# A gated recurrence and a two-way maxout layer on one core: three directly loaded blocks instead of four, single-block chunks, and the first stores sent later

## The chip, the core and the metric

The kernel runs on one core of one Trainium2 chip. Its time is the device time of one execution in microseconds (us). The kernel before the change has a median of 397.41 us over five runs, which lie between 396.77 and 397.58.

A core has five engines with a queue of instructions each: TensorE (PE in the profile, with the loading of weights as PEld), VectorE (DVE), ScalarE (ACT), GpSimd (POOL) and SyncE (SP, which here only issues DMAs). Each works through its queue in order and waits where an operand isn't there yet.

## What is computed

```python
sig = 1 / (1 + exp(-f_logit))
f = lower_bound + (1 - lower_bound) * sig        # 4 x 6144 x 256
for t in range(6144):
    h = f[:, t] * h + (1 - f[:, t]) * x[:, t]
    y[:, t] = h
out = maximum(y @ w1, y @ w2) @ w_out            # w1, w2: 256 x 1024, w_out: 1024 x 256
```

All inputs and the output are float32. The recurrence runs over the tokens of each of the four batches and each of 256 channels by itself. The second part works token by token on 24576 tokens.

## The kernel before

**Arithmetic.** The maximum is written as `relu(y @ (w2 - w1)) @ w_out + y @ (w1 @ w_out)`, so that each token needs one hidden product instead of two. With `u = sigmoid(-f_logit)` the forget factor is `1 - (1 - lower_bound) * u`, and the input of the recurrence is `u * x`; the factor `1 - lower_bound` is put into the weights. The prepared weights are `wd` (the difference), `wob` (`w_out` in bf16) and `w13` (the product of `w1` and `w_out`).

**Blocks.** A block is 512 tokens; there are 48, twelve in each batch. The recurrence wants the channels on the partitions and the tokens along the free dimension, so both inputs have to be turned. A block then needs: `u` by ScalarE (gate), `v = u * x` by VectorE (drive), the forget factors for two halves of 128 channels (forget), a scan for each half on VectorE, eight hidden products of 128 units (each two matmuls with 512 columns), eight relus on ScalarE, and the projection, 40 matmuls with 256 columns, with copies and stores of the result in two pieces.

**Two ways in.** The first `NP = 4` blocks are loaded as float32 by SP (`load`), gated and driven in their natural layout, and turned by TensorE (`turn_pe`, 16 transposes for a block). All later blocks go in chunks of `CB = 2` blocks. `cast` makes a bf16 copy of f_logit and of x in one of two scratch buffers in DRAM, with two DMAs issued on POOL. `turn_dma` reads them back turned, with two transposing DMAs on SP, into tiles of 2 x 1024 elements in each partition. `cast_behind` puts one small POOL copy from the turned f into `held`, which waits for that turn, and issues the next chunk's cast behind it. So casts and turns of successive chunks form one chain.

**Order.** Nothing reorders the work: the order in the source is the order in each engine's queue. `LOADS` is the order of the loads. `PLAN` is the hand-written prologue. Its items are: G gate, V drive, TU and TV turns on TensorE, F forget, S scan, RW and RO rounding of weights, D difference, SC scaling, TW and KW turns of w1, W and KL the product `w13`, H hidden, R relu, P a step of the projection, L its linear steps, O copy out, `warm` products that only keep TensorE busy; then the block and unit, the half of the block (a or b), and behind a dot the engine. `CA` at its end issues chunk 0, and the cast of chunk 1 behind it. Outputs of the prologue are copied by O and sent by `send_pending` as soon as chunk 0's turns have been issued.

The loop follows, for blocks j from 3 to 48 and eight steps fc: the hidden product of block j, and an eighth of the projection of block j - 1. At (j, 0) and (j, 4) `store` copies and sends a piece of an earlier block. At the places in `gate_of` the recurrence of a later block is put in, and at those in `turn_of` a chunk's turns and the next cast.

SP's queue therefore holds the loads, the first turns, and then stores and turns in the order of the loop; a turn behind a store waits until VectorE has made that store's copy.

Of the kernel before, what the change touches and what calls it, by code (L numbers as in the profile page):

```python
# [16 lines left out]
def kernel(  # L17
# [22 lines left out]
    NQ = TB // P  # L40
    NBB = S // TB
    NBLK = B * NBB
    NP = 4
    CB = 2
    assert NBB % CB == 0 and NP % CB == 0
    NCH = (NBLK - NP) // CB
    NS = 2

    const = ctx.enter_context(tc.tile_pool(name="const", bufs=1))
# [8 lines left out]
    midpool = ctx.enter_context(tc.tile_pool(name="mid", bufs=2))  # L58
    ypool = ctx.enter_context(tc.tile_pool(name="ypool", bufs=4))
    rpool = ctx.enter_context(tc.tile_pool(name="rpool", bufs=3 * FC))  # L60
    opool = ctx.enter_context(tc.tile_pool(name="opool", bufs=8))
    lastpool = ctx.enter_context(tc.tile_pool(name="last", bufs=2))
    PS = bass.MemoryType.PSUM
    ps_d = ctx.enter_context(tc.tile_pool(name="ps_d", bufs=5, space=PS))
# [100 lines left out]
    }  # L165

    def cast(c):
        b, k = divmod(NP + c * CB, NBB)
        for name, src in (("fs", f_logit), ("xs", x)):
            nc.gpsimd.dma_start(  # L170
                out=spare[c % NS, name][:],
                in_=src[b, k * TB : (k + CB) * TB, :],
                max_dma_last_dim=4096,
            )

    def turn_dma(c):
        for s, name in enumerate(("fs", "xs")):
            t = ttpool.tile([P, KC, CB * TB], BF16, name=("fT", "xT")[s])
            turned[c, s] = t
            nc.sync.dma_start_transpose(out=t[:], in_=spare[c % NS, name][:])  # L180

    def cast_behind(c):

        if c + 1 < NCH:
            last = CB * TB - 1
            nc.gpsimd.tensor_copy(out=held[:], in_=turned[c, 0][:, KC - 1, last : last + 1])  # L186
            cast(c + 1)

    def part(j, s):
        c, o = divmod(j - NP, CB)  # L190
        return turned[c, s][:, :, o * TB : (o + 1) * TB]

    def gate(j):
# [125 lines left out]
    def send_out(j, g):  # L319
        r0 = j * TB + 2 * g * P  # L320
        nc.sync.dma_start(
            out=out[r0 : r0 + 2 * P, :].rearrange("(p r) d -> p r d", r=2),
            in_=osbs[j, g][:],
        )

    def store(j, g):
        copy_out(j, g)
        send_out(j, g)

    def store_row(j, g, r):  # L330
        osb = lastpool.tile([P, D], FP32, name="row")
# [111 lines left out]


    LOADS = """
    f0a x0a f0b w13 w23 x0b w12 w22 wo3 w10 w20 w11 wo2 w21 f1a x1a wo0 f1b x1b wo1
    f2a f2b x2a x2b f3 x3
    """
    PLAN = """
    G0a RW3.p keeps_T keeps V0a TU0a D31.p warm3 TV0a D30.p G0b F0a0.v warm4 TU0b  # L450
    D21.p F0a1.v S0a1 S0a0 V0b F0b1.a warm1 TW3 F0b0.a RW0.p warm5 TV0b RW2.v S0b1
    D01.p KW3.a TW2 SC31.a SC30.a KW2.a S0b0 RO3.a H06a H07a D20.v SC21.a warm3 H06b
    SC20.v H07b D00.v W133 RW1.v R07.a TW0 H04b H04a RO2.p H05a R06.a P071 SC00.v
    H05b P070 P061 D10.p TW1 SC01.a KW0.v R05.a R04.v H01a KW1.v H00a H00b H01b P040
    P050 P060 G1a P041 SC10.v V1a W132 R01.a D11.p TU1a RO0.p SC11.a P051 TV1a R00.a
    H02a F1a1.v F1a0.a RO1.p H03b S1a1 P011 G1b H02b S1a0 P010 H03a R02.a W130 V1b
    P001 R03.a TU1b H17a F1b1.v P000 TV1b H15a F1b0.a S1b1 S1b0 G2a H16a P031 P030
    P021 G2b W131 KL1.v TU2a F2a0.a P020 H17b H15b KL0.v H16b L01 L11 R17.a TU2b
    H10a H10b R16.a V2a R15.v F2a1.v H11b O01.a P161 H11a TV2a F2b0.a H12b P151 L10
    P171 V2b H12a R11.a F2b1.v R10.a S2a1 TV2b S2a0 G3b P150 R12.a S2b1 G3a L00 S2b0  # L460
    H13a V3b TU3b O00.a H13b P101 R13.a F3b1.v H14a P160 F3b0.v H14b P100 P170 H20
    H26 V3a TU3a P111 F3a1.v H21 R14.a H27 R20.a F3a0.v R26.a TV3a S3a1 P120 H24
    TV3b R21.a P121 P110 S3a0 H22 R27.a S3b1 P130 R24.a R22.a S3b0 H23 P131 R23.a
    H25 P140 O10.v P141 R25.a O11.v CA
    """

    engines = {"a": nc.scalar, "v": nc.vector, "p": nc.gpsimd}
# [10 lines left out]

    outs = []

    def send_pending():

        while outs and turned:
            send_out(*outs.pop(0))

    def issue(item):
        name, _, e = item.partition(".")
        eng, on_dve, on_act = engines.get(e), e == "v", e == "a"
        kind = name.rstrip("0123456789ab")
        arg = ["ab".index(c) if c in "ab" else int(c) for c in name[len(kind) :]]  # L490
        if kind == "warm":
            keep_warm(arg[0])
        elif name == "keeps_T":
            turn_bound()
        elif name == "keeps":
            keeps()
        elif kind in ("G", "V") and len(arg) == 2:
            (gate_nat if kind == "G" else drive_nat)(arg[0], 2 * arg[1], 2 * arg[1] + 2)
        elif kind in ("TU", "TV"):
            turn_pe(arg[0], "UV".index(kind[1]), arg[1])  # L500
        elif kind == "F" and len(arg) == 3:
            j, x, h = arg
            tok = slice(x * HB, (x + 1) * HB)
            forget(ffs[j][:, h, tok], uT[j, x][:, h, :], h, on_act)
        elif kind == "S" and len(arg) == 3:
            j, x, h = arg
            scan(j, h, x * HB, (x + 1) * HB, vT[j, x][:, h, :])
        elif kind == "RW":
            round_w1(arg[0], eng)
        elif kind == "RO":  # L510
            round_wout(arg[0], eng)
        elif kind == "D":
            diff(arg[0], arg[1], eng)
        elif kind == "SC":
            scale(arg[0], arg[1], on_dve)
        elif kind == "TW":
            turn_w1(arg[0])
        elif kind == "KW":
            keep_w1(arg[0], eng)
        elif kind == "W":  # L520
            linear_weights(int(name[3]))
        elif kind == "KL":
            keep_linear(arg[0], on_dve)
        elif kind == "H":
            (hidden_half if len(arg) == 3 else hidden_whole)(*arg)
        elif kind == "R":
            relu(arg[0], arg[1], on_dve)
        elif kind == "P":
            pair_steps(arg[0], arg[2], [arg[1]])
        elif kind == "L":  # L530
            pair_steps(arg[0], arg[1], [FC, FC + 1])
        elif kind == "O":
            copy_out(arg[0], arg[1], on_act)
            outs.append(arg)
            send_pending()
        elif kind == "CA":
            nc.gpsimd.tensor_copy(out=held[:], in_=ins[2][1][:, 3, D - 1 : D])
            cast(0)
            turn_dma(0)
            cast_behind(0)  # L540
            send_pending()
        else:
            raise ValueError(item)


    turn_of = {(3, 5): 1, (5, 2): 2, (7, 0): 3}
    turn_of |= {divmod(FC * (NP + c * CB - 3) - 3, FC): c for c in range(4, NCH)}
    gate_of = {(3, 1): 4, (3, 6): 5, (4, 5): 6, (5, 3): 7, (6, 3): 8, (7, 1): 9}
    gate_of |= {(b - 2, 4): b for b in range(10, NBLK)}

    with tc.manual_schedule():
        for j in range(NP):
            alloc_in(j)
        nc.scalar.dma_start(out=lbr[:], in_=lower_bound.rearrange("(h p) -> h p", p=P))
        for name in LOADS.split():
            load_item(name)
        nc.vector.memset(warm[:], 0.0)  # L557
        make_identity(nc, ident[:])
        nc.vector.tensor_copy(out=ident_b[:], in_=ident[:])
        keep_warm(7)  # L560
        for item in PLAN.split():
            issue(item)
        assert not outs

        for j in range(3, NBLK + 1):
            for fc in range(FC):
                if j < NBLK:
                    hidden(j, fc)
                project(j - 1, fc)
                if fc == 0 and j > 3:  # L570
                    store(j - 2, 1)
                if fc == 4 and j < NBLK:
                    store(j - 1, 0)
                if j == NBLK and fc in (3, 5, 7):
                    if fc == 3:
                        store(j - 1, 0)
                    else:
# [41 lines left out]
```

## Time and profile before

The page describes one profiled execution on this core. That execution took 396.93 us; its span, from the first to the last instruction, is 395.2 us. A digit in a row of tenths is the busy share in a fortieth of the span.

| what | value |
|---|---|
| median of five runs | 397.41 us (396.77 to 397.58) |
| profiled execution | 396.93 us, span 395.2 us |
| granted TensorE clock | full in every stretch |
| bytes moved by DMA | 79.12 MB, mean 200 GB/s |
| plain DMAs and turns from SP (q1) | 56.9% of 16 engines' span |
| casts from POOL (q0) | 35.6% of 16 engines' span |

```profile
PE   7999999999999999999999999999999999999996
PEld 3896766667777776767777776767777776666775
DVE  4896875757755765676567556755775576567622
ACT  4787676676667666766776677667666766676661
POOL 2511011101001101101101011011011010100000
PEclk9999999999999999999999999999999999999999
DMA  7999999989999999999989999999898898981122
...
L240 ACT ACTIVATE rt<-dT 128x512 bf16<-128x512 f32 x382 | 223.1, 596 | 105.2 <-PE dT L245 102.1
L268 PE MATMUL psO<-wob,rt 128*128 128x256 bf16 x1536 | 231.0, 273 | 0.2
...
L245 PE MATMUL dT<-y,wd 128*128 128x512 bf16 x690 | 208.8, 379 | 2.2
L149 DVE TENSOR_TENSOR_SCAN y<-ff,y,v 128x512 bf16<-128x512 bf16 x82 | 105.2, 1283 | 2.9
```

In a row of a group stand the line, the engine, the operation, the tile written and those read, the count, then busy us and mean ns of one, and the idle time before them with what ended it. TensorE's rows show almost no idle time before them; those of ScalarE and VectorE do, and they wait for TensorE. The DMA row is high from the start until near the end.

### The profile page before, as it was taken

The page shows a single profiled execution, that of the slowest core. Times are in us where ns is not written, and L with a number is a line of the kernel's source. Part 1 is how long each engine was busy: PE and PEld are TensorE (multiplying, and loading weights), DVE is VectorE, ACT ScalarE, POOL GpSimd, SP SyncE. Part 2 cuts the span into 40 slices and gives each one's busy share as a digit, 9 for nine tenths or more (in the row PEclk, how much of TensorE's full clock was granted, in tenths as well). Part 3 has the DMA queues.
Part 4 walks back from the last instruction along what each step waited for, and adds up shares of the span by engine and source line. Part 5 has one row for each costly group of instructions (what it writes and reads, how often), then busy time and mean ns, then how long its engine had stood idle before and what let it go on. Part 6 is the DMA issues. An engine that isn't in the chain of part 4 may idle for free.

```text
span 395.2 us, 7146 instructions
## 1 busy us (share of the span) xinstructions
PE 387.2 (98%) x2793; PEld 274.4 (69%) x2840; DVE 251.5 (64%) x366; ACT 273.5 (69%) x451; POOL 37.7 (10%) x83
## 2 busy tenths in 40 slices
PE   7999999999999999999999999999999999999996
PEld 3896766667777776767777776767777776666775
DVE  4896875757755765676567556755775576567622
ACT  4787676676667666766776677667666766676661
POOL 2511011101001101101101011011011010100000
PEclk9999999999999999999999999999999999999999
DMA  7999999989999999999989999999898898981122
GB/s 249 350 244 196 225 219 197 247 182 204 210 230 219 212 221 224 226 234 192 207 197 208 182 219 189 223 216 188 199 211 205 187 201 196 216 188 55 53 81 107
DMA packets 125078, 79.12 MB, mean 200 GB/s; under 512 B 94194, under 2 KB 101620, under 8 KB 125044
## 3 DMA queue, kind: packets, MB, share of 16 engines
q1 hardware_dynamic: 113072, 55.59, 56.9%
q0 software_dynamic: 11968, 23.07, 35.6%
q8 instruction: 22, 0.36, 0.4%
q14 instruction: 12, 0.10, 0.1%
q10 hardware_dynamic: 4, 0.00, 0.0%
HBM read 53.48 MB, written 48.23 MB: 257 GB/s over the span
## 4 chain that ended last, share of the span: by engine, by line
PE 95%; DMA 1%; DVE 1%; issue 1%; SPq 1%; DVEq 0%
PE psO L268 53%; PE dT L245 39%; PE dT L225 2%; DMA xn<-in_x_dram 1%; PE dT L126 1%; SPq L100 0%; PE psO L413 0%; DVE vn L113 0%; SPq L344 0%; DVE y L149 0%; DVE wd L388 0%; DVE wdf L380 0%; DVE row L332 0%; PE dT L396 0%; DVEq L113 0%
## 5 line engine op out<-in xcount | busy, mean ns | idle before, releaser
L240 ACT ACTIVATE rt<-dT 128x512 bf16<-128x512 f32 x382 | 223.1, 596 | 105.2 <-PE dT L245 102.1
L268 PE MATMUL psO<-wob,rt 128*128 128x256 bf16 x1536 | 231.0, 273 | 0.2
L268 PEld LDWEIGHTS <-rt 128*128 128x128 bf16 x1536 | 150.0, 98 | 94.7
L245 PE MATMUL dT<-y,wd 128*128 128x512 bf16 x690 | 208.8, 379 | 2.2
L149 DVE TENSOR_TENSOR_SCAN y<-ff,y,v 128x512 bf16<-128x512 bf16 x82 | 105.2, 1283 | 2.9
L317 DVE COPY osb<-psO 128x512 f32<-128x512 f32 x93 | 62.7, 679 | 67.4 <-PE psO L268 67.4
L245 PEld LDWEIGHTS <-wd 128*128 128x128 bf16 x736 | 72.0, 98 | 8.7
L268 PE MATMUL psO<-w,y 128*128 128x256 bf16 x384 | 72.5, 273 | 0.0
L201 DVE TENSOR_TENSOR v<-u,xT 128x1024 bf16<-128x1024 bf16 x44 | 30.5, 692 | 60.7 <-ACT u L197 52.6
L197 ACT ACTIVATE u<-fT 128x1024 bf16<-128x1024 bf16 x44 | 46.2, 1049 | 1.9 <-DMA fT<-fs 1.9
L268 PEld LDWEIGHTS <-y 128*128 128x128 bf16 x384 | 37.6, 98 | 4.4
L186 POOL CAST held<-fT 128x1 f32<-128x1 bf16 x21 | 5.4, 256 | 279.9 <-DMA fT<-fs 279.9
L138 DVE TENSOR_SCALAR ff<-u,nom 128x512 bf16<-128x512 bf16 x88 | 29.7, 338 | 0.0
L170 POOL DMA_DIRECT2D fs<-in_f_logit_dram x22 | 12.3, 559 | 4.7 <-issue 4.7
L170 POOL DMA_DIRECT2D xs<-in_x_dram x22 | 12.2, 552 | 0.0
L149 DVE TENSOR_TENSOR_SCAN y<-nff,y,dT 128x256 bf16<-128x256 bf16 x14 | 9.6, 731 | 1.8 <-PE dT L126 1.3
L225 PE MATMUL dT<-y,wd 128*128 128x256 bf16 x64 | 10.1, 273 | 0.3 <-DVE wd L388 0.2
L433 PE MATMUL psO<-warm 128*128 128x512 bf16 x22 | 7.2, 459 | 1.2 <-DVE warm L557 1.2
L149 DVE TENSOR_TENSOR_SCAN y<-ff,v 128x512 bf16<-128x512 bf16 x6 | 7.3, 1225 | 0.2
L108 ACT ACTIVATE un<-fn 128x512 bf16<-128x512 f32 x8 | 5.0, 627 | 3.1 <-DMA fn<-in_f_logit_dram 2.9
L113 DVE TENSOR_TENSOR vn<-un,xn 128x512 bf16<-128x512 bf16 x8 | 6.1, 759 | 1.2 <-DMA xn<-in_x_dram 1.2
L225 PEld LDWEIGHTS <-wd 128*128 128x128 bf16 x64 | 5.8, 98 | 1.4 <-issue 0.4
(40 smaller groups left out, 51.2 us busy)
## 6 DMA issues: line engine op xcount, KB each, us to landing
out_dram<-osb SPq DMA_DIRECT2D x95, 256.0 KB, 3.0
fs<-in_f_logit_dram POOLq DMA_DIRECT2D x22, 512.0 KB, 6.4
xs<-in_x_dram POOLq DMA_DIRECT2D x22, 512.0 KB, 9.4
fn<-in_f_logit_dram SPq DMA_DIRECT2D x6, 256.0 KB, 6.0
xn<-in_x_dram SPq DMA_DIRECT2D x6, 256.0 KB, 5.6
w1n<-in_moe_w_dram SPq DMA_DIRECT2D x4, 256.0 KB, 5.6
w2n<-in_moe_w_dram SPq DMA_DIRECT2D x4, 256.0 KB, 5.9
won<-in_moe_w_out_dram SPq DMA_DIRECT2D x4, 256.0 KB, 6.0
```

The costliest lines, as they stand in the source:

```text
L113: nc.vector.tensor_tensor(out=vs[j][:, q0:q1, :], in0=us[j][:, q0:q1, :], in1=ins[j][1][:, q0:q1, :], op=ALU.mult,)
L138: nc.vector.tensor_scalar(out=o, in0=i, scalar1=nom[:, h : h + 1], scalar2=1.0, op0=ALU.mult, op1=ALU.add)
L149: nc.vector.tensor_tensor_scan(out=ys[j][:, h, t0:t1], data0=ffs[j][:, h, t0:t1], data1=v, initial=initial, op0=ALU.mult, op1=ALU.add,)
L170: nc.gpsimd.dma_start(out=spare[c % NS, name][:], in_=src[b, k * TB : (k + CB) * TB, :], max_dma_last_dim=4096,)
L197: nc.scalar.activation(out=us[j][:], in_=part(j, 0), func=AF.Sigmoid, scale=-1.0)
L201: nc.vector.tensor_tensor(out=vs[j][:], in0=us[j][:], in1=part(j, 1), op=ALU.mult)
L225: nc.tensor.matmul(dts[j, fc][:, tok], lhsT=wd[:, kc, unit(fc)], rhs=ys[j][:, kc, tok], start=(first and kc == 0), stop=(not first and kc ...
L240: nc.scalar.activation(out=rt[:], in_=dts[j, fc][:], func=AF.Relu)
L245: nc.tensor.matmul(dts[j, fc][:], lhsT=wd[:, kc, unit(fc)], rhs=ys[j][:, kc, :], start=(kc == 0), stop=(kc == KC - 1),)
L268: nc.tensor.matmul(ps, lhsT=lhsT, rhs=rhs, start=start, stop=stop, skip_group_check=True)
L317: nc.vector.tensor_copy(out=osbs[j, g][:], in_=pos[j, g, 0][:])
L433: nc.tensor.matmul(idle[:].rearrange("p r d -> p (r d)"), lhsT=warm[:, 0:P], rhs=warm[:], start=True, stop=True,)
```

## The change

- `NP` becomes 3. Block 3 is no longer loaded and turned by TensorE; it goes the way of the later blocks.
- `CHUNKS` lists the chunks: blocks 3, 4 and 5 as chunks of one block, then pairs from (6, 7) on. `cast`, `turn_dma` and `cast_behind` take the number of blocks from it. A single's turns fill the first 512 of the 1024 columns of their tile.
- `CA` now stands within `PLAN`, waits for x of block 1 and issues the cast and turns of chunk 0. `CB`, later in `PLAN`, issues the cast of chunk 1 behind them, and its turns. Behind `PLAN`, chunks 2 and 3 are cast and turned, and the cast of chunk 4 is issued, each behind the turned f of the chunk before.
- No store is sent in the prologue or at j = 3 and 4. The copies are put in a list, and from j = 5 on `send_pending` sends up to two of the oldest at (j, 0) and (j, 4). The pool of output tiles grows from 8 to 12.
- `LOADS` and `PLAN` are new orders. `turn_of` and `gate_of` are new for the first chunks. Chunks from (10, 11) on are turned at the same places in the loop as before.

```diff
-    NP = 4
+    NP = 3
     CB = 2
...
+    CHUNKS = [(NP + i, 1) for i in range(CB * 2 - 1)]
+    CHUNKS += [(b, CB) for b in range(2 * NP, NBLK, CB)]
...
-    opool = ctx.enter_context(tc.tile_pool(name="opool", bufs=8))
+    opool = ctx.enter_context(tc.tile_pool(name="opool", bufs=12))
...
     def cast(c):
-        b, k = divmod(NP + c * CB, NBB)
+        b0, n = CHUNKS[c]
+        b, k = divmod(b0, NBB)
         for name, src in (("fs", f_logit), ("xs", x)):
             nc.gpsimd.dma_start(
-                out=spare[c % NS, name][:],
-                in_=src[b, k * TB : (k + CB) * TB, :],
+                out=spare[c % NS, name][0 : n * TB, :],
+                in_=src[b, k * TB : (k + n) * TB, :],
                 max_dma_last_dim=4096,
             )
...
-            nc.sync.dma_start_transpose(out=t[:], in_=spare[c % NS, name][:])
+            nc.sync.dma_start_transpose(
+                out=t[:, :, 0 : n * TB], in_=spare[c % NS, name][0 : n * TB, :]
+            )
...
     def store(j, g):
         copy_out(j, g)
-        send_out(j, g)
+        outs.append((j, g))
...
     LOADS = """
+    f0a x0a w12 f0b x0b w22 w10 w20 wo2 w13 w23 w11 wo0 w21 f1a x1a f1b wo3 x1b wo1
+    f2 x2
     """
     PLAN = """
+    keeps_T D20.p G0a V0a TU0a warm1 TV0a RW2.a warm6 TW2 keeps G0b F0a0.v warm1
+    TU0b F0a1.v KW2.a F0b1.a S0a0 S0a1 V0b warm3 TV0b F0b0.a D21.v SC21.a SC20.a
+    RW0.a D00.p S0b1 D01.p S0b0 warm6 H04a RW3.p RO2.v H05a SC00.a H04b H05b R04.a
...
+    R02.a W133 KW1.a RO1.v P060 F1b0.a P071 CA TV1b S1b0 H14a H16a F1b1.a H13a W131
+    H15a KL1.a P020 S1b1 G2a G2b P031 P030 P021 H14b KL0.v CB H16b TU2a R14.v H13b
...
+    O01.a H17b P111 P151 H12b G3 P100 S2a0 S2b1 H12a P110 P130 L10 S2b0 V3 R17.a H24
+    R12.a R24.a H22 R22.a H20 H27 F31.v H23 R20.a F30.v S31 P140 H21 S30 H26 P120
+    R27.a R21.a P121 H25 R23.v P171 R26.a P160 R25.v P170 O10.v O11.a
     """
...
         elif kind == "CA":
-            nc.gpsimd.tensor_copy(out=held[:], in_=ins[2][1][:, 3, D - 1 : D])
+            nc.gpsimd.tensor_copy(out=held[:], in_=ins[1][1][:, 3, D - 1 : D])
             cast(0)
             turn_dma(0)
+        elif kind == "CB":
             cast_behind(0)
-            send_pending()
+            turn_dma(1)
...
-    turn_of = {(3, 5): 1, (5, 2): 2, (7, 0): 3}
...
-    gate_of = {(3, 1): 4, (3, 6): 5, (4, 5): 6, (5, 3): 7, (6, 3): 8, (7, 1): 9}
-    gate_of |= {(b - 2, 4): b for b in range(10, NBLK)}
+    turn_of = {(6, 0): 4, (7, 4): 5, (9, 2): 6}
+    turn_of |= {divmod(FC * (CHUNKS[c][0] - 3) - 3, FC): c for c in range(7, NCH)}
+    gate_of = {(3, 1): 4, (4, 1): 5, (5, 2): 6, (6, 1): 7, (7, 0): 8, (7, 5): 9}
+    gate_of |= {(8, 7): 10} | {(b - 2, 4): b for b in range(11, NBLK)}
...
+        for c in range(1, 4):
+            cast_behind(c)
+            if c < 3:
+                turn_dma(c + 1)
...
+                if j > 4 and fc in (0, 4):
+                    send_pending(2)
```

More of the change, by code (lines that the diff above doesn't have):

```diff
@@ L42 @@
     NBLK = B * NBB
-    NP = 4
+    NP = 3
     CB = 2
-    assert NBB % CB == 0 and NP % CB == 0
-    NCH = (NBLK - NP) // CB
+    CHUNKS = [(NP + i, 1) for i in range(CB * 2 - 1)]
+    CHUNKS += [(b, CB) for b in range(2 * NP, NBLK, CB)]
+    assert NBB % CB == 0
+    NCH = len(CHUNKS)
     NS = 2
@@ L176, in turn_dma @@
     def turn_dma(c):
+        n = CHUNKS[c][1]
         for s, name in enumerate(("fs", "xs")):
@@ L179, in turn_dma @@
             turned[c, s] = t
-            nc.sync.dma_start_transpose(out=t[:], in_=spare[c % NS, name][:])
+            nc.sync.dma_start_transpose(
+                out=t[:, :, 0 : n * TB], in_=spare[c % NS, name][0 : n * TB, :]
+            )
     def cast_behind(c):
         if c + 1 < NCH:
-            last = CB * TB - 1
+            last = CHUNKS[c][1] * TB - 1
             nc.gpsimd.tensor_copy(out=held[:], in_=turned[c, 0][:, KC - 1, last : last + 1])
             cast(c + 1)
+    home = {b + o: (c, o) for c, (b, n) in enumerate(CHUNKS) for o in range(n)}
     def part(j, s):
-        c, o = divmod(j - NP, CB)
+        c, o = home[j]
         return turned[c, s][:, :, o * TB : (o + 1) * TB]
@@ L445 @@
     LOADS = """
-    f0a x0a f0b w13 w23 x0b w12 w22 wo3 w10 w20 w11 wo2 w21 f1a x1a wo0 f1b x1b wo1
-    f2a f2b x2a x2b f3 x3
+    f0a x0a w12 f0b x0b w22 w10 w20 wo2 w13 w23 w11 wo0 w21 f1a x1a f1b wo3 x1b wo1
+    f2 x2
     """
     PLAN = """
-    G0a RW3.p keeps_T keeps V0a TU0a D31.p warm3 TV0a D30.p G0b F0a0.v warm4 TU0b
-    D21.p F0a1.v S0a1 S0a0 V0b F0b1.a warm1 TW3 F0b0.a RW0.p warm5 TV0b RW2.v S0b1
-    D01.p KW3.a TW2 SC31.a SC30.a KW2.a S0b0 RO3.a H06a H07a D20.v SC21.a warm3 H06b
@@ L453 @@
[L453 to L464, printed above, removed]
+    keeps_T D20.p G0a V0a TU0a warm1 TV0a RW2.a warm6 TW2 keeps G0b F0a0.v warm1
@@ new lines @@
+    TU0b F0a1.v KW2.a F0b1.a S0a0 S0a1 V0b warm3 TV0b F0b0.a D21.v SC21.a SC20.a
+    RW0.a D00.p S0b1 D01.p S0b0 warm6 H04a RW3.p RO2.v H05a SC00.a H04b H05b R04.a
+    W132 SC01.v R05.a TW0 H01b D31.v KW0.a H00a TW3 H00b D30.p SC31.v R00.a H01a
+    P040 SC30.v P051 P050 KW3.v P041 R01.a RO0.p D10.p H07a D11.v H06a G1a RW1.p
+    H06b RO3.p SC11.v W130 H07b P000 P010 R07.a TU1a SC10.v P001 V1a H03a H03b TV1a
+    F1a1.v R06.a TW1 H02b G1b F1a0.v H02a S1a0 P011 R03.a V1b TU1b S1a1 P061 P070
+    R02.a W133 KW1.a RO1.v P060 F1b0.a P071 CA TV1b S1b0 H14a H16a F1b1.a H13a W131
@@ L465 @@
+    H15a KL1.a P020 S1b1 G2a G2b P031 P030 P021 H14b KL0.v CB H16b TU2a R14.v H13b
+    V2a L01 R16.a F2a0.v H15b R13.a P141 H10b R15.a TU2b V2b F2b0.a L00 H10a H11b
+    R10.a F2a1.v TV2a O00.v F2b1.a L11 H17a H11a TV2b P131 P150 P101 P161 S2a1 R11.a
+    O01.a H17b P111 P151 H12b G3 P100 S2a0 S2b1 H12a P110 P130 L10 S2b0 V3 R17.a H24
+    R12.a R24.a H22 R22.a H20 H27 F31.v H23 R20.a F30.v S31 P140 H21 S30 H26 P120
+    R27.a R21.a P121 H25 R23.v P171 R26.a P160 R25.v P170 O10.v O11.a
     """
@@ L479, with send_pending @@
     outs = []
-    def send_pending():
-        while outs and turned:
+    def send_pending(n):
+        for _ in range(min(n, len(outs))):
             send_out(*outs.pop(0))
@@ L534, in issue @@
             outs.append(arg)
-            send_pending()
         elif kind == "CA":
-            nc.gpsimd.tensor_copy(out=held[:], in_=ins[2][1][:, 3, D - 1 : D])
+            nc.gpsimd.tensor_copy(out=held[:], in_=ins[1][1][:, 3, D - 1 : D])
             cast(0)
             turn_dma(0)
+        elif kind == "CB":
             cast_behind(0)
-            send_pending()
+            turn_dma(1)
+        elif kind == "G":
+            gate(arg[0])
+        elif kind == "V":
+            drive(arg[0])
+        elif kind == "F":
+            forget_half(arg[0], arg[1], on_act)
+        elif kind == "S":
+            scan_half(*arg)
         else:
             raise ValueError(item)
-    turn_of = {(3, 5): 1, (5, 2): 2, (7, 0): 3}
-    turn_of |= {divmod(FC * (NP + c * CB - 3) - 3, FC): c for c in range(4, NCH)}
-    gate_of = {(3, 1): 4, (3, 6): 5, (4, 5): 6, (5, 3): 7, (6, 3): 8, (7, 1): 9}
-    gate_of |= {(b - 2, 4): b for b in range(10, NBLK)}
+    turn_of = {(6, 0): 4, (7, 4): 5, (9, 2): 6}
+    turn_of |= {divmod(FC * (CHUNKS[c][0] - 3) - 3, FC): c for c in range(7, NCH)}
+    gate_of = {(3, 1): 4, (4, 1): 5, (5, 2): 6, (6, 1): 7, (7, 0): 8, (7, 5): 9}
+    gate_of |= {(8, 7): 10} | {(b - 2, 4): b for b in range(11, NBLK)}
     with tc.manual_schedule():
@@ L562 @@
             issue(item)
-        assert not outs
+        for c in range(1, 4):
+            cast_behind(c)
+            if c < 3:
+                turn_dma(c + 1)
         for j in range(3, NBLK + 1):
@@ L576 @@
                         store(j - 1, 0)
+                        send_pending(2)
                     else:
```

## The prediction

> **What bounds the kernel now.** I read the busy shares first, then the chain of waits by engine, then TensorE by stretches, and last the time line of the two DMA issuing queues. The page says:
>
> ```profile
> span 395.2 us, 7146 instructions
> PE 387.2 (98%) x2793; PEld 274.4 (69%) x2840; DVE 251.5 (64%) x366; ACT 273.5 (69%) x451; POOL 37.7 (10%) x83
> ...
> PE 95%; DMA 1%; DVE 1%; issue 1%; SPq 1%; DVEq 0%
> ```
>
> TensorE is busy for 98% of the span and is 95% of the chain: time can be won only by taking TensorE work away or starting earlier, and is lost wherever TensorE is made to wait. The stretches show where there is anything to win (time, then TensorE busy; granted clock, DMA share and GB/s at the end):
>
> ```profile
> 0.00:10.00 10.00, 7.89 (x41) 3.13 (x41) 4.62 (x11) 4.81 (x8) 2.83 (x10) 1.00 0.78 250
> 10.00:20.00 10.00, 9.64 (x96) 8.21 (x96) 8.85 (x16) 7.71 (x15) 5.22 (x8) 1.00 1.09 350
> 20.00:30.00 10.00, 10.00 (x104) 8.98 (x103) 9.02 (x19) 8.25 (x16) 1.41 (x3) 1.00 1.03 242
> ```
>
> From 20 us on TensorE never stops, at full clock. Three times on its time line serve as marks: the first useful hidden product (H06a) starts at 10.27, the loop (block 3, unit 0) at 35.63, and block 6 at
>
> ```profile
> 59.09 0.59 PE L245 MATMUL dT<-y,wd 128*128 128x512 bf16 x2
> ```
>
> 59.09 - 35.63 = 23.46 is three loop passes of 7.82 us. If TensorE reaches block 6 at time T, everything after it shifts by T - 59.09: from there on both kernels run the same matmuls, and the tail is the same.
>
> The DMA side is what the change leans on. The first chunk's cast and turns, on the POOL and SP queues:
>
> ```profile
> 23.13 0.73 POOL L170 DMA_DIRECT2D fs<-in_f_logit_dram  x1
> ...
> 34.19 0.19 POOL L186 CAST held<-fT 128x1 f32<-128x1 bf16 x1 [9.78 <-DMA fT<-fs]
> 34.63 0.55 POOL L170 DMA_DIRECT2D fs<-in_f_logit_dram  x1 [0.26 <-issue]
> ...
> 28.25 3.36 SPq L180 DMA_TRANSPOSE fT<-fs  x1
> 31.93 2.24 SPq L180 DMA_TRANSPOSE xT<-xs  x1
> ```
>
> and the DMA answers at these issues (last number: us from issue to landing), plus that of a turn at 87.42 that had no cast beside it:
>
> ```profile
> fs<-in_f_logit_dram POOLq DMA_DIRECT2D x1, 512.0 KB, 5.1
> ...
> fT<-fs SPq DMA_TRANSPOSE x1, 5.8
> ...
> xT<-xs SPq DMA_TRANSPOSE x1, 4.3
> ...
> fT<-fs SPq DMA_TRANSPOSE x1, 4.5
> ```
>
> The reader is to see a serial chain: cast, then turn, then the POOL copy into `held`, which waits for the turned f and only then lets the next cast out. One pair takes 31.93 + 4.3 - 23.13 = 13.1 us from its cast's issue to its turned x. There is slack now, since four blocks are loaded directly: block 6 has its last scan behind it at 55.84, 3.25 us ahead of 59.09.
>
> **TensorE work and start.** Block 3 no longer goes through TensorE: 16 transposes go. Four of them advance TensorE by 0.23 us (24.06 to the next product at 24.29), so 16 are 0.91 us, all on the path. Of warm-up, 22 products become 24 (at 0.216 us each, 0.4 more), but the three at 10.92, after the first useful product, are gone: 0.65 less on the path. One w1 turn (0.23 us) moves behind the start. From the first hidden product to the loop: 10.27 to 35.63 is 25.36 us now, of which 24.7 are products and 0.66 waits; then 24.7 - 0.91 - 0.65 + 0.23 = 23.4.
>
> The start moves little. Loads land about 0.74 us apart (SP issues one whenever an earlier one lands: 12.09, 12.83). x0b moves from sixth to fifth, but the first products now need w22, still eighth, at about 8.4 to 9.1: its two differences (POOL 0.73, DVE about 0.4) and two scalings on ScalarE (0.5 each, behind one another) end near 10.3. So first product 10.3; with waits of about 0.5 us (0 to 1.5) the loop starts at 10.3 + 23.4 + 0.5 = 34.2, and TensorE could reach block 6 at 34.2 + 23.46 = 57.7: **a gain of 1.4 us, if the blocks are ready**.
>
> **Edits that cost nothing.** Block 3 exchanges four half scans (0.73 each) for two whole ones (1.28): DVE and ScalarE gain slightly and have room in the loop (a block's two scans, two forgets, drive and two copies are 5.3 of 7.82 us). Stores held back: twelve output buffers instead of eight cover the eight copies waiting at (5,0); nothing on TensorE waits for a store while buffers last. In SP's queue all four first turns now stand ahead of every store; before, turn 1 stood behind five stores that waited for DVE copies (34.26 to 43.6). That removes a real hold of SP. Two more chunks are four more casts, four more turns, 0.55 us of POOL each, idle time there. Chunks from (10,11) on are issued as far ahead of their use as before.
>
> **The new wait: the chain of chunks up to block 6.** The order is now block 3, 4, 5, then pair (6,7), each cast behind `held`. No row shows a single-block cast or turn, so from both sides:
> - Cast: a pair's f takes 5.1. Between 25 and 30 us only casts move, at 182 to 215 GB/s (mean 205), so half of 512 KB is 1.3 us less: 3.8. Upper end 5.1 (nothing saved), lower 3.2. The lower one is the Trainium skill's price, "DMA: Bandwidth & Descriptors", section "Anatomy of one DMA": about 2.0 us plus bytes over 436 GB/s. With the 1 MB that a pair's f reads it gives 4.4 where the trace shows 5.1; I keep the row, since by the rule three casts would come 1.8 us earlier.
> - Turn: a pair's f without a cast beside it takes 4.5, of which SP's issue is 2.28. A single's x cast is done about when the turn begins to move, so I start from this row. Half the issue: 3.4. Upper end 4.5 (nothing saved), lower 2.3 (everything halved).
> - A rule speaks against the single turns. The same page, section "Latency and other measured facts", gives DMA transposes 261 GB/s where the middle dimension is non-contiguous and 350-400 where it is contiguous, some 30% off. Every turn in the trace fills its whole tile; a single fills `t[:, :, 0:512]` of a 1024-wide tile, two separate pieces per partition. The rows' full tiles (512 KB in an issue of 2.0 to 2.3 us) run no faster than the slow figure, so the rule may be spent already: then 3.4. By the rule the moving 1.1 us become 1.1 / 0.7 = 1.6, and the turn 3.9. No row has this form; the two lie close, and I take 3.7 between them.
>
> Now the sum. x1b (19th load in both) must land just before wo1, whose user on POOL was released at 18.86: about 18.2; first cast issued 18.4. Its f lands 3.8 + 0.4 (the last loads still move until about 21) later, 22.6; turned f at 26.3, turned x about 1.2 later. ScalarE reaches G3 when 6.1 us of products remain to the loop, about 28.1: **block 3 is in time**. From a turned f to the next cast takes 0.6 (34.05 to 34.63). So a single's cycle is 0.6 + 3.8 + 3.7 = 8.1: turned f of block 4 at 34.4 (its gate stands at 34.2 + 1.95 = 36.2: in time), of block 5 at 42.5 (gate at 44.0: in time). The pair's cast is issued at 43.1, and its circumstances are those of the first chunk of the trace, no store in flight and x's cast beside f's turn: turned x at 43.1 + 13.1 = 56.2. Drive, two forgets and two scans: 4.0 us (turned x at 51.87, last scan over at 55.84 in the trace). Block 6 is ready at **60.2**, not 57.7.
>
> So a wait of 2.5 us at block 6 takes the place of what was won: 60.2 - 59.09 = 1.1 us longer. TensorE's own 2.5 us lead does not help, because this chain hangs on x1b and DMA alone. By the row alone (turn 3.4) block 6 would be ready at 59.3, 0.2 us longer than before; by the rule alone (3.9) at 60.8, 1.7 longer.
>
> Behind it: six stores go out at once after turn 3 and meet the cast of (8,9). The nearest row, 34.63, with five stores beside: f 7.1, then a turn of 6.2 and x by 8.1 after its start. Cast at 54.6, turned x 69.9, block 8 ready 73.9; TensorE there at 60.2 + 15.64 = 75.8. No second wait.
>
> **Against the measurement.** The profiled execution took 396.93 us, 1.73 around its span; 1.1 more is 398.03. The median of the five runs lies 0.48 above it: 398.5. A change below about 0.2% (0.8 us) can't be told from none.
>
> **Rivals.**
> - *The chunks arrive in time.* Needs turned x of (6,7) by 53.7, that is 0.8 us less in each of three cycles: for it speaks SP free of stores, against it that every pair's f turn beside a cast took 5.8 or more in the early rows. The full gain of 1.4: 396.0. Faster begins where block 6 is ready before 58.3.
> - *A tie.* Ready at 58.3 to 59.9, as with the row's turn of 3.4: 397.6.
> - *Singles cost as much as pairs, or the stores do.* A cast of 4.3 and a turn of 4.1 add 0.9 in each of three cycles, 2.7 us: 401.2; the full upper ends add 2.2 each, 6.6: 405. If six stores and a cast stretch f to the 9.4 us of the row at 92.49, block 8 is about 2.3 us later, 76.2, only 0.4 past 75.8; it adds little.
>
> **How the numbers follow.** Forecast slower by about 1.1 us: 0.4; the dear singles 0.1; tie 0.22; in time, wholly or in part, 0.28. Slower 0.5, same 0.22, faster 0.28. The signs are divided, so the likeliest case's own range is 398.2 to 399.8; the whole goes from TensorE's floor, 395.9, to 400.9 with singles 0.8 us dearer a cycle than I take.
>
> **What would show it.** Right: TensorE without a stop up to block 5, then one wait for DVE's scan of block 6 of 1.5 to 3.5 us; the loop's first product near 34.2; turned f of the singles about 8 us apart. Wrong: no gap at block 6 (singles cheaper), gaps at blocks 3 to 5 (dearer), or a loop start past 36, where waits in the hand-written order would decide instead.

## The result, and the profile after

The changed kernel has a median of 399.25 us over 25 runs, against 397.41 us over 43 runs of the kernel before: a ratio of 1.0046, with a 95% interval of 1.0035 to 1.0057. It is **slower by about 1.8 us**. Its runs are also far less alike: they lie between 396.95 and 401.57, those of the kernel before between 396.62 and 397.97.

The profiled execution took 397.66 us, so it is one of the shorter ones. Its page:

```profile
span 395.9 us, 7107 instructions
PE 386.8 (98%) x2779; PEld 273.4 (69%) x2825; DVE 251.1 (63%) x363; ACT 273.0 (69%) x450; POOL 39.4 (10%) x87
...
PE 73%; DMA 23%; issue 1%; ACT 1%; POOL 0%; SPq 0%; DVE 0%; POOLq 0%; ACTq 0%
```

TensorE is as busy as before, and the busy shares alone would show nothing. The chain by engine does: DMA was 1% of the chain that ended last, and is now 23%. That share is no cost by itself: the chain is followed back from the last late block, and here that leads to the first cast. The same chain in order of time, from its first cast to where it meets ScalarE (start, duration, what):

```profile
18.91 5.64 DMA fs<-in_f_logit_dram
24.57 3.54 DMA fT<-fs
...
28.68 3.47 DMA fs<-in_f_logit_dram
32.17 3.02 DMA fT<-fs
...
35.76 3.53 DMA fs<-in_f_logit_dram
39.31 3.39 DMA fT<-fs
...
43.27 5.02 DMA fs<-in_f_logit_dram
...
48.43 4.80 DMA fT<-fs
...
53.80 7.75 DMA fs<-in_f_logit_dram
...
61.69 6.81 DMA fT<-fs
...
69.06 8.32 DMA fs<-in_f_logit_dram
...
77.52 7.57 DMA fT<-fs
...
85.66 6.51 DMA fs<-in_f_logit_dram
...
92.31 5.51 DMA fT<-fs
...
97.92 1.06 ACT u L206
```

Cast, turn, cast, turn from the first cast to the gate of block 12, with 0.6 us at most between a landing and the next issue: nothing but its own transfers holds this chain back, so it can't make up for a late one. The reader should also see the jump from 5.02 to 7.75 and 8.32: those are the casts of (8,9) and (10,11).

On TensorE's time line the loop starts 0.85 us earlier (the first row is of the kernel before, the second of the changed one):

```profile
35.63 0.59 PE L245 MATMUL dT<-y,wd 128*128 128x512 bf16 x2
...
34.78 0.60 PE L254 MATMUL dT<-y,wd 128*128 128x512 bf16 x2
```

Then come three waits in the changed kernel, which the first number of a row's bracket or the distance to the row before shows:

```profile
58.25 0.38 PE L254 MATMUL dT<-y,wd 128*128 128x512 bf16 x1
59.34 0.38 PE L254 MATMUL dT<-y,wd 128*128 128x512 bf16 x1 [0.71 <-DVE y L152]
...
91.21 0.70 PE L277 MATMUL psO<-wob,rt 128*128 128x256 bf16 x5 [0.21 <-DVE osb L326]
...
100.00 0.77 PE L277 MATMUL psO<-wob,rt 128*128 128x256 bf16 x3
```

The first is block 6's second scan (two such products stand 0.22 apart elsewhere, here 1.09: 0.87 lost). It came late because VectorE had waited for the turned x of (6,7):

```profile
55.45 0.69 DVE L210 TENSOR_TENSOR v<-u,xT 128x1024 bf16<-128x1024 bf16 x1 [4.13 <-DMA xT<-xs]
```

The second is a copy of a result out of `psO` that VectorE made late, because it had stood behind the recurrence of block 10 (0.38 lost against the usual spacing). The third row stretches over relus that ScalarE made late, since its queue had waited 2.00 us for the turned f of (12,13) (0.28 lost). With the earlier start the sum is -0.85 + 0.87 + 0.38 + 0.28 = 0.68, and the span has grown by 0.7. So in this execution the account closes. At block 6 saving and loss are even, and the rest is lost behind it; the median execution loses some 1.6 us more, which this trace can't show.

### The profile page after: what moved, and what is told of

Same layout as the page of the kernel before. It is cut to its first block, busy times and chain, and to the rows that moved or that the text cites. A ratio compares the mean times of both kernels' runs of the same rounds, so it can differ in the third digit from the quotient of the medians.

```text
span 395.9 us, 7107 instructions
## 1 busy us (share of the span) xinstructions
PE 386.8 (98%) x2779; PEld 273.4 (69%) x2825; DVE 251.1 (63%) x363; ACT 273.0 (69%) x450; POOL 39.4 (10%) x87
## 4 chain that ended last, share of the span: by engine, by line
PE 73%; DMA 23%; issue 1%; ACT 1%; POOL 0%; SPq 0%; DVE 0%; POOLq 0%; ACTq 0%
PE psO L277 42%; PE dT L254 32%; DMA fs<-in_f_logit_dram 10%; DMA fT<-fs 9%; DMA xn<-in_x_dram 2%; DMA w2n<-in_moe_w_dram 2%; DMA w1n<-in_moe_w_dram 1%; ACT rt L249 0%; POOL held L193 0%; ACT u L206 0%; SPq L103 0%; DVE row L341 0%; SPq L185 0%; POOL held L544 0%; POOLq L193 0%
## 5 line engine op out<-in xcount | busy, mean ns | idle before, releaser
L152 DVE TENSOR_TENSOR_SCAN y<-ff,y,v 128x512 bf16<-128x512 bf16 x84 | 107.7, 1283 | 2.9
L206 ACT ACTIVATE u<-fT 128x1024 bf16<-128x1024 bf16 x45 | 47.2, 1049 | 5.0 <-DMA fT<-fs 4.8
L174 POOL DMA_DIRECT2D fs<-in_f_logit_dram x24 | 13.3, 554 | 4.9 <-issue 4.9
L174 POOL DMA_DIRECT2D xs<-in_x_dram x24 | 13.1, 548 | 0.0
L152 DVE TENSOR_TENSOR_SCAN y<-nff,y,dT 128x256 bf16<-128x256 bf16 x10 | 6.9, 733 | 0.3
L116 DVE TENSOR_TENSOR vn<-un,xn 128x512 bf16<-128x512 bf16 x6 | 4.1, 687 | 4.0 <-DMA xn<-in_x_dram 4.0
L442 PEld LDWEIGHTS <-warm 128*128 128x128 bf16 x24 | 2.4, 110 | 3.6 <-issue 1.4
## 6 DMA issues: line engine op xcount, KB each, us to landing
xs<-in_x_dram POOLq DMA_DIRECT2D x21, 512.0 KB, 10.3
```

The source lines that it names most:

```text
L152: nc.vector.tensor_tensor_scan(out=ys[j][:, h, t0:t1], data0=ffs[j][:, h, t0:t1], data1=v, initial=initial, op0=ALU.mult, op1=ALU.add,)
L174: nc.gpsimd.dma_start(out=spare[c % NS, name][0 : n * TB, :], in_=src[b, k * TB : (k + n) * TB, :], max_dma_last_dim=4096,)
L206: nc.scalar.activation(out=us[j][:], in_=part(j, 0), func=AF.Sigmoid, scale=-1.0)
L442: nc.tensor.matmul(idle[:].rearrange("p r d -> p (r d)"), lhsT=warm[:, 0:P], rhs=warm[:], start=True, stop=True,)
```

## The experiments

In each diff the lines with a minus are those of the changed kernel, `...` marks what is left out, and a "single" is a chunk of one block. Times are medians; the kernel before was run beside each (397.34 to 397.49), and ratios are to it.

### What the change saves when no block can be late

```diff
     def cast(c):
+        if 1 <= c <= 6:
+            return
...
     def turn_dma(c):
...
+            if 1 <= c <= 6:
+                turned[c, s] = turned[0, s]
+                continue
```

> The changed kernel with chunks 1 to 6 neither cast nor turned; the gates and drives of blocks 4 to 11 read chunk 0's turned tile again, so these blocks are computed from block 3's inputs. TensorE does all its work, but no block from 4 to 11 can be late. It measures what the change saves before any wait: loop start 0.85 us earlier than before in the changed kernel's trace, so 396.4 to 396.7, with a spread as narrow as before's. If the serial chain is not what costs, the time stays near 399.

Chunks 1 to 6 are the blocks 4 to 13, so two blocks more than the expectation names read block 3's inputs. Measured: 396.56 us (396.11 to 397.09), ratio 0.9978 (0.9968 to 0.9987). The saving is real, 0.87 us at the median (this kernel is called floor below), and the spread is as narrow as before's. The change therefore loses 399.25 - 396.56 = 2.7 us at the median, all of it through casts and turns of chunks 1 to 6, or what they and the other transfers do to each other.

### The stores left out

```diff
     def send_out(j, g):
+        if j < 12:
+            return
```

> The changed kernel without the stores of blocks 0 to 11, so those rows of the output are not written. Theory (the stores kept back until after turn 3 come out in bursts of six beside the casts of (8,9) and (10,11), stretch these from about 5 to 8 us, and that makes blocks 10 and 12 late): those two casts' f back at 5 to 5.7 us, turned f of (10,11) near 78 instead of 85, only the wait of about 0.9 us at block 6 left, 397.0 to 397.8. Rival (pair chunks are too slow by themselves): casts stay above 7 us, waits at blocks 10 and 12 stay, 399 or more.

Measured: 397.54 us (396.38 to 401.57), ratio 1.0013 (0.9994 to 1.0031). The two casts' answers, with the last number the us from issue to landing, first of (8,9), then of (10,11):

```profile
fs<-in_f_logit_dram POOLq DMA_DIRECT2D x1, 512.0 KB, 5.4
...
fs<-in_f_logit_dram POOLq DMA_DIRECT2D x1, 512.0 KB, 5.1
```

In the changed kernel they took 7.8 and 8.3. Turned f of (10,11) came at 79.29 instead of 85.12, and no wait of TensorE is left behind block 6. The stores of blocks 0 to 11 are thus needed to make the later blocks late, and at the median they are worth 399.25 - 397.54 = 1.7 of the 2.7 us. Without them the change comes out even with the kernel before. The run leaves out all stores of that stretch and not only those kept back; that it is their coming in bursts is tested only by the spread stores further down.

The profiled execution of this kernel was one of its long ones (399.98 us) and happens to show one source of the spread. Its first f turn took

```profile
fT<-fs SPq DMA_TRANSPOSE x1, 5.2
```

where the changed kernel's took 3.5. It landed at 30.70 instead of 28.07, every later landing up to block 6 was 2.6 to 3.1 us late with it, and TensorE waited 0.7 us at block 5 and 2.1 at block 6. A delay at the start of the chain was handed on to its end. Why the first turn took longer in this execution is not shown.

### The hold of the stores undone

```diff
-        outs.append((j, g))
+        send_out(j, g)
...
-    turn_of = {(6, 0): 4, (7, 4): 5, (9, 2): 6}
+    turn_of = {(3, 5): 2, (4, 6): 3, (6, 0): 4, (7, 4): 5, (9, 2): 6}
...
-        for c in range(1, 4):
-            cast_behind(c)
-            if c < 3:
-                turn_dma(c + 1)
+        cast_behind(1)
+        send_pending(len(outs))
```

> The changed kernel with the hold of the stores alone undone: turns 2 and 3 stand in the loop at (3,5) and (4,6), and each store goes out as soon as its copy is made. Theory (holding back buys an undisturbed chain up to block 6 and pays for it behind): the cast of block 5 and that of (6,7) are stretched by 1 to 2 us each, block 6 is ready 2 to 4 us later than 59.2, and the later chunks gain little; 399.5 to 402. Rival (the hold is what costs): block 6 as now, no late waits, 397 to 398.

Measured: 404.98 us (404.38 to 405.65, four runs), ratio 1.0188 (1.0175 to 1.0201). The direction was right and the size too small. The cast of block 5 took 5.6 us instead of 3.5, its turn was issued 1.3 us after that, behind a store on SP, and took 5.0 instead of 3.4. Turned x of (6,7) came at 61.52 instead of 55.33. TensorE lost 2.2 us at block 5 and 4.7 at block 6, whose two products are these:

```profile
63.95 0.39 PE L254 MATMUL dT<-y,wd 128*128 128x512 bf16 x1 [3.23 <-DVE y L152]
65.51 0.59 PE L254 MATMUL dT<-y,wd 128*128 128x512 bf16 x1 [1.17 <-DVE y L152]
```

So with three loaded blocks the hold is worth some 6 us; it moves the stores to where they cost less.

### The stores spread, and the chain started earlier

```diff
                 if j > 4 and fc in (0, 4):
-                    send_pending(2)
+                    send_pending(2 if fc == 0 or j > 10 else 1)
```

> The changed kernel with the kept-back stores sent three instead of four to a block until block 10 (two at step 0, one at step 4): five, four and five stores instead of six, six and four stand between turns 3, 4, 5 and 6 on SP's queue. Theory (bursts of six stores stretch the casts of (8,9) and (10,11)): their f back after 6 to 7.3 us instead of 7.8 and 8.3, turned f of (10,11) 1 to 2 us earlier than 85.1, the block 6 wait as it is, median 398.0 to 398.8. Rival (the later waits come from the chain's late start alone): no change, 399.25.

Measured: 398.72 us (396.81 to 401.52), ratio 1.0036 (1.0022 to 1.0050). The casts took 6.9 and 7.2 us, turned f of (10,11) came at 82.68, and behind block 6 no wait is left in its trace; that at block 6 is 1.20 us. The interval overlaps that of the changed kernel, so a gain at the median isn't settled by this alone.

```diff
-    P040 SC30.v P051 P050 KW3.v P041 R01.a RO0.p D10.p H07a D11.v H06a G1a RW1.p
+    P040 SC30.v P051 P050 KW3.v P041 R01.a RO0.p D10.p H07a D11.v H06a G1a RW1.p CA
...
-            nc.gpsimd.tensor_copy(out=held[:], in_=ins[1][1][:, 3, D - 1 : D])
+            nc.gpsimd.tensor_copy(out=held[:], in_=ins[1][0][:, 1, D - 1 : D])
```

> The changed kernel with CA moved up in PLAN to behind RW1 and waiting for the first half of f of block 1 instead of x of block 1: the chain's first cast is issued near 16.8 instead of 18.9, while loads still move. Theory (TensorE's waits at blocks 6, 10 and 12 all hang on one chain whose start sets every later landing): turned f of block 3 near 26 instead of 28.1, block 6 ready 1.5 to 2 us earlier, no wait there, those at 10 and 12 smaller; 396.5 to 398.0. Rival (the last loads are delayed as much as the chain gains, and the prologue then waits for x of blocks 1 and 2): loop start later than 35.5, 398.5 to 400.

Measured: 398.27 us (397.08 to 400.65), ratio 1.0027 (1.0018 to 1.0037). The reason given fell: the first cast was issued at 16.99 instead of 18.91, but took 7.4 us beside the loads instead of 5.6, and the turned f came at 27.95, where it had come at 28.07. The block 6 wait is still 0.81 us in its trace. Why the median fell all the same, by 1 us with intervals that just touch, is not shown by a trace of one execution.

> Both edits, the earlier first cast and the stores three to a block. If the chain is the only cost of the change, this comes nearest to the kernel without a late block: 396.4 to 397.3, faster than before. If either edit only moves the contention elsewhere, 398 or more.

Measured: 397.85 us (396.84 to 399.85), ratio 1.0018 (1.0009 to 1.0028). The two together take more than half of the loss back, clear of the changed kernel's interval, but the kernel stays behind the one before. Its trace has no wait at or behind block 6, but one of 1.3 us in the prologue, for the drive of a loaded block, which had waited 2.48 us for its x.

### The split destination of a single turn

```diff
-            t = ttpool.tile([P, KC, CB * TB], BF16, name=("fT", "xT")[s])
+            pool = ttpool if n > 1 else t1pool
+            t = pool.tile([P, KC, n * TB], BF16, name=("fT", "xT")[s])
```

> The changed kernel with the single turns written to tiles of their own, 2 x 512, so that each fills its tile. Theory (the split destination is what makes a single's issue 1.23 to 1.33 us where half of a pair's is 1.0 to 1.15): issue 1.0 to 1.15 us, turned f of block 5 some 0.3 to 0.5 us earlier, time 0 to 0.5 us less than 399.25. Rival (a fixed part of the issue, whatever the destination): issue times and block 6 unchanged.

Measured: 399.44 us (397.67 to 401.18), ratio 1.0047 (1.0035 to 1.0059), the same. The issues of the single turns of f (those of x took 1.22 to 1.25):

```profile
24.52 1.34 SPq L187 DMA_TRANSPOSE fT<-fs  x1
...
32.13 1.26 SPq L187 DMA_TRANSPOSE fT<-fs  x1
...
39.83 1.23 SPq L187 DMA_TRANSPOSE fT<-fs  x1
```

In the changed kernel all six took 1.23 to 1.33. The form of the destination costs nothing here: the slower rate of the Trainium skill that the prediction weighed ("DMA: Bandwidth & Descriptors", section "Latency and other measured facts") does not show in a single turn into a part of its tile. The trace of this kernel, as slow as the changed one, is that of an execution of 398.10 us, and TensorE lost 1.01 us at block 6, then 0.18 and 0.47 at the same two places behind it.

### Casts that don't wait for the turn

If the serial chain costs, letting casts run beside turns should help. Five kernels tried which, the first with the casts of chunks 1 to 4 released from the wait:

```diff
-            nc.gpsimd.tensor_copy(out=held[:], in_=turned[c, 0][:, KC - 1, last : last + 1])
+            if c >= 4:
+                nc.gpsimd.tensor_copy(out=held[:], in_=turned[c, 0][:, KC - 1, last : last + 1])
```

> The changed kernel, but the casts of chunks 1 to 4 are issued without the POOL copy that waits for the turned f of the chunk before; a cast then waits only until the turn before last has read its scratch buffer. Theory (the serial chain cast, turn, next cast sets when blocks 6, 10 and 12 are ready): turned f of block 5 some 7 us earlier than 42.7, the pair (6,7) turned by about 48, no wait of TensorE at block 6, and of the changed kernel's 1.84 us over the one before at least the 0.9 us of that wait goes; 396.5 to 398.3. Rival (the DMA engines are full, and a cast that runs beside a turn only stretches both): casts of 5 to 7 us for a single, block 6 no earlier, 399 or more.

Measured: 403.90 us (403.22 to 404.85, five runs), ratio 1.0166 (1.0153 to 1.0179). My theory fell in this form. Block 5's f came at 41.27, only 1.4 us earlier where 7 were expected, and the x turn of (6,7), issued at 44.71, met the cast of (8,9), whose x was issued at 45.33, and from 50.07 on six stores:

```profile
xT<-xs SPq DMA_TRANSPOSE x1, 15.5
```

In the changed kernel it takes 4.4. Block 6 was ready at about 64.2 instead of 59.3. The question became which cast may run beside which turn. With `c >= 2` (called free2 below) and with `c >= 3` (free3) in place of `c >= 4`:

> The changed kernel with only the casts of chunks 1 and 2 (blocks 4 and 5) released from the POOL copy; those of (6,7) and later stay behind it. In the run with four released casts the late block was 6, and only because its own x turn took 15.5 us beside the cast of (8,9); up to there the chain ran 1.4 to 5 us ahead. If that is right: turned f of block 5 near 40 to 41.5, block 6 ready 1 to 2.5 us earlier than 59.2, no or little wait there, 397.0 to 398.5. If overlap of casts and turns is bad everywhere: 399 or more.

Measured: 397.17 us (396.41 to 398.73), ratio 0.9994 (0.9984 to 1.0004): turned f of block 5 at 37.70, turned x of (6,7) at 51.86, no wait at block 6 or later, but one of 0.7 us for block 3.

> The same with the cast of (6,7) released too, and that of (8,9) held behind turn 3 as in the changed kernel, so that no cast of a pair runs beside the turn of a pair. If the serial chain is the change's only cost: (6,7) turned by about 49 instead of 55.3, no wait of TensorE at blocks 6, 10 and 12, near the kernel without late blocks, 396.5 to 397.2, faster than before. If released casts cost as much as they win: 399 to 404.

Measured: 396.99 us (396.08 to 398.48), ratio 0.9990 (0.9981 to 0.9999). (6,7) was turned at 52.7, not at 49. This is the only kernel here that computes and stores everything and whose interval lies below 1, by 0.1% and hardly clear of it, so no gain that a user would notice. But it takes 2.3 of the 2.7 us back with all stores in place: its casts of (8,9) and (10,11) still took 9.1 and 7.7 us in its trace, and no block behind 3 was late there. So the stores cost only where the chain reaches them without a lead, and their 1.7 us can't be added to a cost of the chain as if the two were apart. Its profiled execution is its longest (398.48), and has one wait left, of 1.6 us, for block 3: the first f turn met the released cast of block 4 and took 6.7 us instead of 3.5 (first row), and ScalarE's relus came late behind the gate of block 3 (second row).

```profile
fT<-fs SPq DMA_TRANSPOSE x1, 6.7
...
33.62 1.08 PE L255 MATMUL dT<-y,wd 128*128 128x512 bf16 x4 [1.41 <-ACT rt L250]
```

That suggested holding chunk 1's cast again and releasing only those of chunks 2 and 3 (`c not in (1, 2)` as the condition), alone (free12) and with the earlier start and spread stores:

> The changed kernel with the casts of chunks 2 and 3 released, and those of chunks 1 and 4 held behind the turned f as before. With chunk 1 released too, its cast stretched the first f turn from 3.5 to 5.2 and 6.7 us and TensorE waited for block 3 (0.7 and 1.6 us). If that is the last wait left: turned f of block 3 at about 28, no wait at blocks 3, 6, 10 and 12, 396.4 to 396.9, within 0.4 us of the kernel without late blocks (396.56). If the later chunks fall back by as much as the first gains: 397 to 398.

Measured: 399.96 us (397.00 to 400.96), ratio 1.0052 (1.0031 to 1.0073).

> The same with the first cast moved up and the stores three to a block. If free12 has no wait left, nothing more is to be had: equal to it within 0.3 us. If its chain is still at times late, this one is 0.3 to 1 us faster than it, and narrower in its spread.

Measured: 398.35 us (396.87 to 403.70), ratio 1.0032 (1.0017 to 1.0047). Both missed. In the trace of free12 the first turn was undisturbed (27.64), but now the cast of block 5 ran beside the turns of block 4, and that of (6,7) beside those of block 5: f of block 4 came at 38.23 instead of 35.17, and x of block 5 took 9.9 us and came at 48.46 instead of 44.52. TensorE waited at blocks 4 and 5 (0.66 and 1.10 us). In free2 and free3 the released cast met the first turns, with block 3 late by 0.7 and 1.6 us, and from there on the chain ran ahead. That an early overlap pays because little is yet due is my reading; it was not tested further.

## Why the prediction was right, and how much of that was luck

| step of the prediction | predicted | in the trace after |
|---|---|---|
| first hidden product | 10.3 | 10.65 |
| waits up to the loop | 0.5 | 0.75, one wait at 12.27 for the rounding of w_out |
| loop start | 34.2 | 34.78 |
| TensorE free for block 6 | 57.7 | 58.25 |
| first cast issued, its f back | 18.4, 22.6 | 18.91, 24.55 |
| cast of f of a single behind the first, turn of f of a single | 3.8, 3.7 | 3.5, 3.0 to 3.5 |
| cycle of a single | 8.1 | 7.1 and 7.5 |
| turned f of blocks 3, 4, 5 | 26.3, 34.4, 42.5 | 28.07, 35.17, 42.71 |
| pair (6,7): cast issued, turned x | 43.1, 56.2 | 43.27, 55.33 |
| block 6 ready | 60.2 | about 59.3 |
| wait at block 6 | 2.5 | 0.87 |
| behind block 6 | no wait | 0.38 and 0.28 |

- **The mechanism was right.** What the prologue saves is real, and it is more than lost on the serial chain of casts and turns. Block 6 waited for DVE's scan as forecast, and no block up to 5 did in the changed kernel's trace.
- **The number came out right by luck in part.** At the medians the forecast is -1.4 saved, +2.5 lost on the chain, and nothing for the stores: +1.1. The runs give -0.87 (floor), +0.98 (397.54 - 396.56, the chain without the stores) and +1.71 (the stores): +1.8. What the prediction took for the cause would by itself have left the time as it was; a term that it put at little brought it into the range.
- **The saving was mis-sized**, 1.4 predicted, 0.85 in the trace and 0.87 at the median of the floor run: the start came 0.35 later and the rounding of w_out made TensorE wait. The start also varies: in the floor run's trace, an execution of 396.86 us, the loop starts at 35.28. The prediction misread one thing on the way: w22 is the sixth load of the new order, not "still eighth". Its time was right (the first difference that needs it began on VectorE at 9.05), but the POOL difference took 0.96 us and not 0.73.
- **The terms of the chain up to block 6 erred against each other.** The first cast, beside the last loads, took 5.6 us and not 4.2. The singles took 7.1 and 7.5 a cycle and not 8.1, as their turns cost about what half a pair's row gave (3.4) or less, and the 0.3 added for the split destination was not there. So the pair's cast was issued only 0.2 us later than forecast. The pair itself took 12.1 us and not 13.1, as its f turn took 4.8 and not 5.8; that, with TensorE 0.55 us later, is why the wait is 0.87 and not 2.5.
- **The step that failed is "No second wait".** It was worked out for block 8 alone, which was indeed in time (turned x of (8,9): 69.9 predicted, 70.52 measured). The chain was not carried on to (10,11): its cast was issued at 69.06 beside the second burst of six stores, took 8.3 us, and turned x came 17.6 us after that issue, more than the 15.64 us that TensorE takes for a pair. The prediction's rival with the stores put this at little; without those stores the median falls by 1.7 us.
- **The prediction took (10,11) for untouched.** It says that chunks from (10,11) on are issued as far ahead of their use as before, and "The change" gives the same places for their turns. By the code the places moved, that of (10,11) from (7,0) to (7,4) and that of (12,13) from (8,5) to (9,2); they are the same only from (14,15) on. The places held nothing up here: the turn of (10,11) was issued 0.1 us behind its cast's landing. But its lead was gone. The turn of f before, with its us from issue to landing:

```profile
71.83 3.37 SPq L180 DMA_TRANSPOSE fT<-fs  x1
...
fT<-fs SPq DMA_TRANSPOSE x1, 5.8
```

It landed at 77.6 before and at 85.1 after, for a block that TensorE reaches at about the same time in both.
- How the median execution shares its loss among blocks 6, 10 and 12 was not seen: of the changed kernel only a short one has been traced.

## What to carry to other kernels

When TensorE's idle time is nearly gone, saving its work in the prologue brings forward the deadline of everything that is fed by DMA; add up the landings of the feeding chain first, and carry the sum on until it has slack again, not only to the first late block. Transfers that are put off come back: count what they meet when they are let go, and whether what they meet still has a lead. A median can hide that a chain has no slack; a spread that grows from 1.3 to 4.6 us, with nothing changed in the engines' busy shares, is a sign of it.

## What the runs showed of the hardware that I had not expected

**A turn beside a cast.** A pair's x turn took 4.4 us with no cast beside it, and 15.5 in the run with four released casts, beside the cast of another pair and then six stores. A single's took 3.3 and 3.9 with no cast beside it in the changed kernel, and 4.6 to 11.1 beside one in the five runs that released casts. The cast lost as well: that of x of (8,9) landed 14.6 us after its issue there, where that of x of (6,7) takes 7.0 in the changed kernel.

```profile
xs<-in_x_dram POOLq DMA_DIRECT2D x1, 512.0 KB, 7.0
...
xs<-in_x_dram POOLq DMA_DIRECT2D x1, 512.0 KB, 14.6
```

Over 50 to 60 us, while that turn was under way, the DMA engines were busier than in the changed kernel and moved half as much (the last two numbers are the DMA share and the GB/s; first the changed kernel, then the run with four released casts):

```profile
50.00:60.00 10.00, 9.24 (x68) 6.47 (x67) 5.45 (x9) 6.39 (x11) 1.28 (x3) 1.00 1.10 231
...
50.00:60.00 10.00, 9.03 (x65) 6.18 (x64) 1.63 (x3) 6.51 (x11) 0.00 (x0) 1.00 1.22 113
```

How much of the 15.5 us is due to the cast and how much to the stores was not taken apart.

**The clock after a wait.** In the run with four released casts TensorE waited for block 6 from about 59 to 64.2, with one product between. The stretches there, with the granted clock as the third number from the end:

```profile
62.00:64.00 2.00, 0.39 (x1) 0.11 (x2) 1.97 (x3) 0.00 (x0) 0.00 (x0) 0.92 1.13 343
64.00:66.00 2.00, 1.80 (x7) 1.01 (x7) 1.32 (x3) 0.60 (x1) 0.00 (x0) 0.50 1.12 242
66.00:68.00 2.00, 1.95 (x11) 1.21 (x11) 0.00 (x0) 1.26 (x2) 1.28 (x3) 0.73 1.20 289
```

After a wait of 3.55 us and one of 1.17 the clock was at half for about 3 us, and a row of five projection matmuls took 1.27 us instead of 0.71. The run with the hold of the stores undone, with waits of 3.23 and 1.17 us, shows the same:

```profile
66.00:68.00 2.00, 2.00 (x9) 1.10 (x8) 0.63 (x2) 0.60 (x1) 0.00 (x0) 0.50 1.07 272
```

The Trainium skill, "TensorE: Matmul & The Clock Gate", section "Part 1: The HAM clock gate", has this as a rule (an idle window of about 3.4 us halves the clock). The rows agree in kind, though in the second run the clock fell with no single wait of that length. The waits of 0.65 and 1.17 us at block 6 in the run without stores left it at full; what lies between was not measured. So in these two runs the late block cost its waits and about 1.4 us more (the sum by which the products after it were late against their usual spacing). Two of the changed kernel's 25 runs, at 400.85 and 401.20 us, have a mean granted clock of 0.996, like these two traces; that a long wait stands behind it there too is likely, but not shown.
